# Sliding-window attention with a gated feed-forward: the last 128 output rows in three pieces instead of two

## The chip, the cores and the metric

The kernel runs on one core of a Trainium2 chip. The time is the device time of one execution in microseconds (us), given as the median of several executions. The profile comes from one execution of its own, and its span (first to last recorded instruction) is a little shorter than that execution's time.

## The reference

Causal attention in a window of 64 positions, for 8 batches, 8 heads, 576 positions and 64 values per head; its output, reordered to 4608 rows (tokens) of 512, goes through a gated feed-forward layer with a hidden width of 1536. Cut to what matters:

```python
scores = np.where((rel >= 0) & (rel < 64), scale * (q @ k.T), -1e9)   # rel: query minus key position
attn = softmax(scores) @ v                                            # per batch and head
x = attn.transpose(0, 2, 1, 3).reshape(4608, 512)
gate = np.maximum(x @ w_gate, 0.0)
val = x @ w_val
out = (gate * val) @ w_out                                            # 4608 x 512, float32
```

## The kernel before, in words

The 4608 rows are cut into ten tiles: four of 384 rows and six of 512. For each tile `t` the kernel computes attention into `xt` (inputs in 16 bits, transposed), then `hidden(t)`, then `output(t)`.

`hidden` runs over the 12 blocks of 128 hidden columns (`NF` = 12): four matmuls with `wg` and four with `wv` for each block (L468). ScalarE applies the ReLU to the first result (L453), VectorE multiplies it by the second into `g_sb` (L456).

`output` runs over the 128-row groups of the tile, called `sub`. For each group one tile `op` of 128 x 512 in PSUM, the accumulator memory, takes 12 matmuls of 512 columns (L482), which add up the 12 hidden blocks. `out_evac` then copies `op` to `o_sb` in SBUF, the working memory, on ScalarE (L489), and SP, an engine that only issues transfers here, starts the store to `out` (L490).

The instruction order on each engine is written out by hand (`tc.manual_schedule()`). A small planner, `Weaver`, keeps a clock that advances with each planned matmul; work on other engines is put in with a due time (`W.at`) and is emitted when the clock gets there. `W.drain()` emits all that is left.

The last of the ten tiles goes through `output_last`: its first three groups as above, then `W.drain()`, then the fourth group, the last 128 rows, in pieces of its own. Before the change there are two pieces of 256 columns, each in an `op` tile of its own with 12 matmuls (L514). The first piece is copied by ScalarE and stored from SP's queue. The second is copied in two halves of 128 columns: one by ScalarE, stored from ScalarE's queue, and one by VectorE, stored from SP's queue (copies L520, stores L521).

Two pools matter. `op` tiles come from `f_ps` under the tag `h`, four banks of PSUM used in turn, together with the `h` tiles of `hidden`. `o_sb` tiles come from `f_sb`, three buffers used in turn: a copy into a buffer has to wait until the store that last read it has landed. The pool `consts`, with one buffer for each name, never reuses a tile.

Of the kernel before, what the change touches and what calls it, by code (L numbers as in the profile page):

```python
# [10 lines left out]
FP32 = mybir.dt.float32  # L11
# [33 lines left out]
def kernel(  # L45
# [10 lines left out]
    nc = tc.nc  # L56
    B, H, S, D = q.shape
    DM = H * D
# [14 lines left out]
    starts = [TT * t for t in range(NS)] + [NS * TT + WT * t for t in range(NL)]  # L73
    widths = [TT] * NS + [WT] * NL

    consts = ctx.enter_context(tc.tile_pool(name="consts", bufs=1))
# [6 lines left out]
    f_sb = ctx.enter_context(tc.tile_pool(name="f_sb", bufs=3))  # L83
# [5 lines left out]
    wo = persist.tile([128, NF, DM], FP16)  # L89
# [403 lines left out]
    def op_tile():  # L493
        return f_ps.tile([128, DM], FP32, name="op", tag="h")

    def output(t, subs=None):
        for sub in range(widths[t] // 128) if subs is None else subs:
            op = op_tile()
            for f in range(NF):
                if f % 4 == 0:  # L500
                    W.advance(W.clock)
                out_mm(t, op, sub, f)
            out_evac(t, op, sub)

    def output_last(t):

        last = widths[t] // 128 - 1
        output(t, range(last))
        W.drain()
        for col in range(2):  # L510
            op = op_tile()
            for f in range(NF):
                g_sb, _ = gs[t]
                nc.tensor.matmul(op[:, 0:256], g_sb[:, f, bass.ds(last * 128, 128)], wo[:, f, 256 * col:256 * col + 256],  # L514
                                 start=(f == 0), stop=(f == NF - 1))
            parts = ((0, 256, nc.scalar.copy, nc.sync),) if col == 0 else (
                (0, 128, nc.scalar.copy, nc.scalar), (128, 256, nc.vector.tensor_copy, nc.sync))
            for c0, c1, copy, queue in parts:
                o_sb = f_sb.tile([128, DM], FP32, name="o_sb")
                copy(o_sb[:, c0:c1], op[:, c0:c1])  # L520
                queue.dma_start(out[bass.ds(starts[t] + last * 128, 128), 256 * col + c0:256 * col + c1], o_sb[:, c0:c1])  # L521

    def output_by_rows(t):
        ops = [op_tile() for _ in range(TT // 128)]
# [8 lines left out]
    with tc.manual_schedule():  # L533
# [134 lines left out]
        for t in range(2, NS + NL):  # L668
            ready(t)
            ahead(t)  # L670
            hidden(t, ((0, widths[t]),))
            (output if t < NS + NL - 1 else output_last)(t)
# [31 lines left out]
```

The softmax here doesn't subtract the row's maximum and nothing guards it: scores larger than these inputs give would overflow.

## Time and profile before

| | |
|---|---|
| time, median of 8 executions | 325.11 us (324.96 to 327.58) |
| the profiled execution, its own time | 325.25 us |
| its span in the profile | 323.5 us |
| mean granted TensorE clock | 0.989 of full |
| busy: TensorE, VectorE, ScalarE, GpSimd | 97%, 59%, 39%, 29% of the span |
| start of the last group's matmuls | 317.40 us |

In the lines of the profile PE is TensorE's matmuls and PEld its weight loads, DVE is VectorE, ACT ScalarE, POOL GpSimd and SP SyncE; a q behind the name is the engine's instruction queue, whose own instructions (issuing a transfer, waiting on a semaphore) are not counted as busy. L514 is line 514 of the kernel. A timeline line gives start, duration, engine, line and operation, then the tiles as out<-in, how many instructions were merged, and in brackets how long the engine had been idle and what released it. The chain is the work that ended last, followed backwards from step to step. A line of issues gives the number of transfers, their size and the time from issue to landing.

### The profile page before, as it was taken

The page shows a single profiled execution, that of the slowest core. Times are in us where ns is not written, and L with a number is a line of the kernel's source. Part 1 is how long each engine was busy: PE and PEld are TensorE (multiplying, and loading weights), DVE is VectorE, ACT ScalarE, POOL GpSimd, SP SyncE. Part 2 cuts the span into 40 slices and gives each one's busy share as a digit, 9 for nine tenths or more (in the row PEclk, how much of TensorE's full clock was granted, in tenths as well). Part 3 has the DMA queues.
Part 4 walks back from the last instruction along what each step waited for, and adds up shares of the span by engine and source line. Part 5 has one row for each costly group of instructions (what it writes and reads, how often), then busy time and mean ns, then how long its engine had stood idle before and what let it go on. Part 6 is the DMA issues. An engine that isn't in the chain of part 4 may idle for free.

```text
span 323.5 us, 8901 instructions
## 1 busy us (share of the span) xinstructions
PE 314.6 (97%) x3851; PEld 169.0 (52%) x3851; DVE 192.0 (59%) x370; ACT 126.9 (39%) x249; POOL 93.6 (29%) x138
## 2 busy tenths in 40 slices
PE   6699999999999999999999999999999999999995
PEld 2585958656556644454445444454445444544443
DVE  5947972587838759564765656673767146723410
ACT  3444325534424523542354234613372237223321
POOL 8766335296800290029100920081000000000000
PEclk9699999999999999999999999999999999999999
DMA  8999998989590079009900892091001200020002
GB/s 217 187 195 210 194 103 175 154 149 163 90 203 4 9 105 190 3 8 125 216 5 4 108 210 18 2 121 71 0 2 37 97 0 2 18 111 6 0 34 98
DMA packets 52488, 29.48 MB, mean 91 GB/s; under 512 B 38880, under 2 KB 43872, under 8 KB 52448
## 3 DMA queue, kind: packets, MB, share of 16 engines
q0 software_dynamic: 46688, 18.29, 48.1%
q1 hardware_dynamic: 5616, 10.55, 9.0%
q8 instruction: 30, 0.49, 0.6%
q14 instruction: 10, 0.08, 0.1%
q10 hardware_dynamic: 144, 0.07, 0.1%
HBM read 37.75 MB, written 9.44 MB: 146 GB/s over the span
## 4 chain that ended last, share of the span: by engine, by line
PE 94%; DMA 2%; POOL 2%; issue 0%; ACT 0%; DVE 0%; DVEq 0%; POOLq 0%
PE h L468 59%; PE op L482 28%; PE st L233 3%; PE pv L371 2%; DMA v<-in_v_dram 2%; PE pv L293 1%; POOL v L191 1%; DMA out_dram<-o_sb 1%; POOL k L167 0%; POOL v L202 0%; POOL v L200 0%; ACT o_sb L489 0%; POOL q L167 0%; PE st L207 0%; POOL ident L107 0%
## 5 line engine op out<-in xcount | busy, mean ns | idle before, releaser
L456 DVE TENSOR_TENSOR g_sb<-r_sb,h 128x512 f16<-128x512 f32 (+1 forms) x120 | 75.3, 630 | 86.5 <-PE h L468 84.8
L468 PE MATMUL h<-xt,wg 128*128 128x512 f16 (+2 forms) x544 | 112.8, 339 | 0.1
L468 PE MATMUL h<-xt,wv 128*128 128x512 f16 (+2 forms) x544 | 111.3, 336 | 0.0
L453 ACT ACTIVATE r_sb<-h 128x512 f32<-128x512 f32 (+1 forms) x120 | 66.7, 558 | 89.8 <-PE h L468 83.9
L482 PE MATMUL op<-wo,g_sb 128*128 128x512 f16 x420 | 93.9, 379 | 0.0
L468 PEld LDWEIGHTS <-wg 128*128 128x128 f16 x544 | 51.9, 99 | 42.7 <-issue 0.6
L468 PEld LDWEIGHTS <-wv 128*128 128x128 f16 x544 | 50.5, 98 | 40.8
L482 PEld LDWEIGHTS <-g_sb 128*128 128x128 f16 x420 | 40.3, 98 | 47.1
L191 POOL DMA_DIRECT2D v<-in_v_dram x41 | 34.6, 863 | 95.1 <-PE pv L371 90.1
L489 ACT COPY o_sb<-op 128x512 f32<-128x512 f32 x35 | 20.5, 585 | 84.7 <-PE op L482 84.5
L356 DVE TENSOR_TENSOR pw<-pw,mask 128x512 f16<-128x512 f16 x48 | 19.3, 422 | 14.7 <-ACT pw L352 14.3
L352 ACT ACTIVATE pw<-st 128x512 f16<-128x512 f32 x48 | 25.7, 607 | 5.0 <-PE st L233 4.7
L200 POOL COPY v<-v 64x512 f16<-64x512 f16 (+1 forms) x21 | 15.4, 732 | 24.0 <-DMA v<-in_v_dram 23.2
L185 DVE STREAM_TRANSPOSE kT<-k 128x576 f32<-128x576 f32 x16 | 19.9, 1246 | 0.2 <-ACT k L178 0.2
L185 DVE STREAM_TRANSPOSE qT<-q 128x576 f32<-128x576 f32 x16 | 19.3, 1237 | 0.1
L267 ACT ACTIVATE p<-st 128x384 f16<-128x384 f32 (+1 forms) x40 | 14.0, 442 | 8.2 <-PE st L233 8.2
L391 DVE TENSOR_TENSOR xw<-pv,rw 128x448 f16<-128x448 f32 (+1 forms) x36 | 16.2, 506 | 0.4
L202 POOL COPY v<-v 64x512 f16<-64x512 f16 (+1 forms) x21 | 15.9, 758 | 1.0
L233 PEld LDWEIGHTS <-kT 32*128 32x128 f16 x1152 | 10.8, 94 | 10.1 <-issue 7.9
L233 PE MATMUL st<-qT,kT 32*128 32x64 f16 x1152 | 12.9, 192 | 3.0 <-DVE qT L185 3.0
L396 DVE STREAM_TRANSPOSE xt<-xw 128x1024 f16<-128x1024 f16 x12 | 14.9, 1244 | 0.4
L272 DVE TENSOR_TENSOR p<-p,mask 128x384 f16<-128x384 f16 x24 | 9.1, 398 | 3.5 <-ACT p L267 3.4
(46 smaller groups left out, 99.0 us busy)
## 6 DMA issues: line engine op xcount, KB each, us to landing
out_dram<-o_sb SPq DMA_DIRECT2D x35, 256.0 KB, 2.7
k<-in_k_dram POOLq DMA_DIRECT2D x15, 288.0 KB, 5.3
q<-in_q_dram POOLq DMA_DIRECT2D x15, 288.0 KB, 7.9
v<-in_v_dram POOLq DMA_DIRECT2D x31, 128.0 KB, 8.7
wg<-in_moe_w_gate_dram POOLq DMA_DIRECT2D x6, 256.0 KB, 6.4
wv<-in_moe_w_val_dram POOLq DMA_DIRECT2D x6, 256.0 KB, 8.2
wo<-in_moe_w_out_dram POOLq DMA_DIRECT2D x3, 512.0 KB, 12.1
v<-in_v_dram POOLq DMA_DIRECT2D x10, 64.0 KB, 6.0
```

The costliest lines, as they stand in the source:

```text
L185: nc.vector.transpose(dst.rearrange("p (i j) -> p j i", i=32)[:, j0:j1], src[:, j0:j1])
L191: nc.gpsimd.dma_start(v16s[b % 2][lo:hi, g, :, 0:64], v[b, :, 64 * g - 64 + lo:64 * g - 64 + hi].rearrange("h p d -> p h d"))
L202: copy(t[0:64, g0:g1:2, h0:h1, 0:64], t[64:128, g0 - 1:g1 - 1:2, h0:h1, 0:64])
L233: return [lambda dh=dh: nc.tensor.matmul(to, kTs[b % 2][rows, hh, 64 * w:64 * w + 128, dh], qTs[b % 2][rows, hh, 64 * w:64 * w + 64, dh], ...
L352: nc.scalar.activation(d["p"][g].rearrange("p n c -> p (n c)"), d["st"][g], ACT.Exp, scale=scale)
L356: nc.vector.tensor_tensor(p, p, mask[:, None, :].to_broadcast([128, 2 * QW, 64]), MUL)
L391: nc.vector.tensor_tensor(d["x"][:, hh, s0:s1], pv[:, :, 0:D].rearrange("p s (c e) -> p s e c", e=2), d["r"][:, hh, s0:s1, :, None].to_bro ...
L453: nc.scalar.activation(part(r_sb), part(h1), ACT.Relu)
L456: nc.vector.tensor_tensor(g_sb[:, f:f + w, c0:c0 + n], part(r_sb), part(h2), MUL)
L468: nc.tensor.matmul(h[:, b * n:b * n + n], wt[:, c, (f + b) * 128:(f + b) * 128 + 128], xt[:, c, c0:c0 + n], start=(c == 0), stop=(c == NC ...
L482: nc.tensor.matmul(op, g_sb[:, f, bass.ds(sub * 128, 128)], wo[:, f], start=(f == 0), stop=(f == NF - 1))
L489: nc.scalar.copy(o_sb, op)
```

## The change

The last 128 rows are computed in three pieces of 256, 128 and 128 columns, 12 matmuls each. The first two are copied whole by ScalarE and stored from SP's queue. The third is copied in two halves of 64 columns: one by ScalarE, stored from ScalarE's queue, one by VectorE, stored from SP's queue. Each of the four copies writes a tile of its own from `consts`, exactly as wide as it is, in place of a part of an `o_sb` buffer.

```diff
         last = widths[t] // 128 - 1
         output(t, range(last))
         W.drain()
-        for col in range(2):
+        for c0, c1 in ((0, 256), (256, 384), (384, DM)):
             op = op_tile()
+            n = c1 - c0
             for f in range(NF):
                 g_sb, _ = gs[t]
-                nc.tensor.matmul(op[:, 0:256], g_sb[:, f, bass.ds(last * 128, 128)], wo[:, f, 256 * col:256 * col + 256],
+                nc.tensor.matmul(op[:, 0:n], g_sb[:, f, bass.ds(last * 128, 128)], wo[:, f, c0:c1],
                                  start=(f == 0), stop=(f == NF - 1))
-            parts = ((0, 256, nc.scalar.copy, nc.sync),) if col == 0 else (
-                (0, 128, nc.scalar.copy, nc.scalar), (128, 256, nc.vector.tensor_copy, nc.sync))
-            for c0, c1, copy, queue in parts:
-                o_sb = f_sb.tile([128, DM], FP32, name="o_sb")
-                copy(o_sb[:, c0:c1], op[:, c0:c1])
-                queue.dma_start(out[bass.ds(starts[t] + last * 128, 128), 256 * col + c0:256 * col + c1], o_sb[:, c0:c1])
+            halves = ((0, n // 2, nc.scalar.copy, nc.scalar), (n // 2, n, nc.vector.tensor_copy, nc.sync))
+            for i, (a0, a1, copy, queue) in enumerate(halves if c1 == DM else ((0, n, nc.scalar.copy, nc.sync),)):
+                o_sb = consts.tile([128, a1 - a0], FP32, name=f"o_last{c0}_{i}")
+                copy(o_sb, op[:, a0:a1])
+                queue.dma_start(out[bass.ds(starts[t] + last * 128, 128), c0 + a0:c0 + a1], o_sb)
```

## The prediction

> **What bounds the kernel now.** I read the page's busy line and its chain first, then the chain of waits and the timeline of the last microseconds, then the stores' times to landing.
>
> ```profile
> PE 314.6 (97%) x3851; PEld 169.0 (52%) x3851; DVE 192.0 (59%) x370; ACT 126.9 (39%) x249; POOL 93.6 (29%) x138
> ...
> PE 94%; DMA 2%; POOL 2%; issue 0%; ACT 0%; DVE 0%; DVEq 0%; POOLq 0%
> ```
>
> TensorE is busy for 97% of the span and makes 94% of the chain that ended last. The change touches only what follows 317.2 us, so the question is how long TensorE's last 24 matmuls take and what runs after them. The chain in order of time, over the last stretch:
>
> ```profile
> 317.60 0.59 ACT o_sb L489
> 318.19 0.02 issue
> 318.21 2.00 DMA out_dram<-o_sb
> 320.20 0.03 issue
> 320.23 0.05 DVEq L520
> ...
> 320.62 0.29 DVE o_sb L520
> ```
>
> The last VectorE copy is tied to a store: the one of the third 128-row group, issued at 318.21 and landed at 320.20. The copy's `o_sb` is the same one of the pool's three buffers. After the landing VectorE's queue works through four semaphore instructions, about 0.1 us apart, and copies at 320.62. The timeline of the same stretch:
>
> ```profile
> 317.18 2.71 PEld L514 LDWEIGHTS <-g_sb 128*128 128x128 f16 x24
> 317.40 2.78 PE L514 MATMUL op<-wo,g_sb 128*128 128x256 f16 x24
> 317.60 0.58 ACT L489 COPY o_sb<-op 128x512 f32<-128x512 f32 x1 [2.00 <-PE op L482]
> 318.95 0.37 ACT L520 COPY o_sb<-op 128x256 f32<-128x256 f32 x1 [0.77 <-PE op L514]
> 319.35 1.92 SPq L521 DMA_DIRECT2D out_dram<-o_sb  x2
> 320.26 0.27 ACT L520 COPY o_sb<-op 128x128 f32<-128x128 f32 x1 [0.94 <-PE op L514]
> 320.56 0.37 ACTq L521 DMA_DIRECT2D out_dram<-o_sb  x1
> 320.62 0.29 DVE L520 COPY o_sb<-op 128x128 f32<-128x128 f32 x1 [10.03 <-ACT o_sb L520]
> ```
>
> TensorE ends at 317.40 + 2.78 = 320.18. ScalarE's copy of the last half runs from 320.26 to 320.53; VectorE's starts only at 320.62, and its bracket names ScalarE's copy as the releaser, not the store. So two things hold it: the store's landing with the semaphores behind it (until 320.57), and ScalarE's copy (until 320.53). A copy released by ScalarE starts some 0.03 us after it elsewhere (ACT L352 from 273.06, 0.61 long by its row's mean, then DVE L356 at 273.69). ScalarE alone would thus have let it start at 320.56: **the buffer's wait costs 0.06 us, not the 10 us in the bracket.** The issues in section order:
>
> ```profile
> out_dram<-o_sb SPq DMA_DIRECT2D x3, 256.0 KB, 2.0
> out_dram<-o_sb SPq DMA_DIRECT2D x1, 128.0 KB, 1.7
> out_dram<-o_sb ACTq DMA_DIRECT2D x1, 64.0 KB, 1.6
> out_dram<-o_sb SPq DMA_DIRECT2D x1, 64.0 KB, 1.7
> ```
>
> SP issues VectorE's half at 320.94 (the second of the merged SPq row: 319.35 + 1.92 - 0.33), which lands at 320.94 + 1.7 = 322.64. ScalarE's half lands at 320.56 + 1.6 = 322.16. The span closes at 323.5, 0.86 after the later one. The end is: TensorE, ScalarE copy, VectorE copy, SP's store, closing.
>
> **What the Trainium skill says.** "PSUM — Partial Sum Buffer", section "PSUM bank collisions raise a hardware error", says that two engines must be kept off one bank at once, two readers included. The trace agrees in kind: the halves share `op` and are copied one after the other. "TensorE: Matmul & The Clock Gate", section "Wait — 56ns, not 53.3ns?", gives N/2.4 + 2.5 ns from one warm matmul to the next, so 55.8 ns for 128 columns. The trace agrees at every width that it has: 192 columns 82.5 ns (below), 512 columns 215.8 (the 36 of L482 from 309.63 to 317.40). The same page, "Back-to-back issue gap", gives about 81 ns for pairs of weight load and matmul at 128 columns; its figure beside that, 131 ns at 512, is not what this trace shows. "DMA: Bandwidth & Descriptors", "Specifications", says that below 512 bytes a transfer does a read-modify-write; no store of before has such short rows.
>
> **The change part by part.**
>
> *Matmuls.* Before, 24 of 256 columns at 109.2 ns (256/2.4 + 2.5): the last starts at 317.40 + 23 x 0.1092 = 319.91 and takes 0.27. After, 12 of 256 columns, then 24 of 128. No 128-column row of this shape exists in the trace. Its nearest rows:
>
> ```profile
> 18.76 2.80 PE L468 MATMUL h<-xt,wv 128*128 128x192 f16 x32
> 21.40 2.76 PE L468 MATMUL h<-xt,wg 128*128 128x384 f16 x16
> ...
> 26.70 0.55 PE L233 MATMUL st<-qT,kT 32*128 32x64 f16 x48
> 27.18 2.77 PE L468 MATMUL h<-xt,wg 128*128 128x384 f16 x16
> ```
>
> The 192-column ones, with a weight load each, come every (21.40 - 18.76)/32 = 82.5 ns, the bare streaming price, although a weight load shows 97 ns: loads overlap each other and hide at 82.5. The L233 ones, 128-column weights on 32 rows, come every 0.48/48 = 10 ns, four row groups in parallel, so one group is reloaded every 40 ns. A load's spacing therefore lies between 40 and 82.5 ns; I take 55.8, streaming. A 128-column matmul lasts about 0.22 (273 ns at 256, 379 at 512, same slope). The end moves to 317.40 + 12 x 0.1092 + 23 x 0.0558 + 0.22 = 320.21: **+0.03 us**. At 82.5 ns it would be +0.64; less than +0.03 is excluded by streaming.
>
> *First and middle pieces.* Columns 0 to 256 run as before: copy 318.95, SP issue 319.35 to 319.68. The middle piece's last matmul ends at 318.71 + 11 x 0.0558 + 0.22 = 319.54; ScalarE, free since 319.32, copies from 319.62 to 319.89 (265 ns), and SP issues from 319.92 to 320.25. That one added copy and one added issue lie under the third piece's matmuls. If that cover went, they would cost 0.27 on ScalarE and 0.33 on SP, which has 0.5 us to spare before its last issue. The added store is 64 KB and lands before the last. Nothing is moved past on other queues, POOL is idle here, and the two later `op` tiles need banks whose copies ended by 315.6.
>
> *Last piece.* ScalarE starts 0.08 after the end, at 320.29. Its copies are 585, 372 and 265 ns at 512, 256 and 128 columns, 0.83 ns a column, so 64 take 0.21: until 320.50, issue at 320.53 (0.03 earlier than before). In the list of waits of the changed program as built, VectorE's copy waits for ScalarE's alone; the waits for eight store semaphores are gone. It starts at 320.53 and takes 0.29 less 64 columns of about 1 ns (L391: 614 ns at 448, 292 at 128), 0.23: until 320.76. SP issues at 320.79, not 320.94: **-0.15 us** including the matmuls' +0.03. Of it 0.06 is the buffer, 0.12 the two narrower copies in series.
>
> *The last store.* Half the bytes, in rows of 256 bytes. 64 KB lands no sooner than 128 KB does (1.7 both on SP, 1.6 on ScalarE's queue), so fewer bytes are worth 0 to -0.1. The read-modify-write: 9 packets an engine of about 25 ns (144 packets are 1.2% of 16 engines over the 19 us queried) are 0.23 us, and a doubling would add as much. Its issue also overlaps ScalarE's by 0.1 us (320.53 to 320.90 against 320.79), where before they just missed. I take +0.05, with -0.1 and +0.3 as ends.
>
> **Sum:** -0.15 + 0.05 = -0.10 us. The profiled execution took 325.25 (span 323.5 and 1.75 around it), so 325.15; the median of the runs is 325.11, 0.14 below, so 325.0.
>
> **The rivals.**
> - *Weight loads set the pace* (slower). For it: LDWEIGHTS shows 97 ns against 55.8, and the skill's 81. Against it: 40 ns in a row group, and full hiding at 192 columns. It turns the gain into a loss from 55.8 + 100/23 = 60 ns a matmul. At 81 ns TensorE ends 23 x 0.025 = 0.58 later than in my sum: 325.6. At 97 ns, 0.95 later: 325.95.
> - *The 256-byte store lands late* (about even). At +0.3 the sum is +0.15: 325.3.
> - *The tail was worth more* (faster). If the 32 KB land 0.3 sooner, as 128 KB do against 256: 324.7. Two copies truly side by side would start VectorE at 320.29 and give another 0.24, but its wait on ScalarE's copy excludes that; so the words "by two engines" do not mean at once, before or after.
> - *It does nothing*: narrower copies and the shorter wait are eaten by the end's fixed 1.7 + 0.86 us: 325.1.
>
> **How the numbers follow.** A measurement of this kernel can tell about 0.3% from no change, 0.98 us; all these cases lie inside. Chances: small gain as worked out, with the case of nothing, 0.60 (324.8 to 325.2); weight loads 0.16; late store 0.12; more gain 0.08; something outside this list, either way, 0.04. The range 324.6 to 325.7 leaves out the worst weight-load case and the unlisted. Faster by over 0.3%: 0.04; slower by over 0.3%: 0.05, mostly weight loads near or above 97 ns; the rest within.
>
> **What would show it.** In the changed profile: 24 matmuls of 128 columns in about 1.5 us, TensorE's end near 320.2; ScalarE copies of 0.21 and VectorE's of 0.23 us, starting 0.03 after ScalarE's ends and with no semaphore instructions of its queue ahead; SP's last issue near 320.8, landing in 1.6 to 1.8; the same 0.86 after. I am wrong if those matmuls take 2 us or more, if VectorE starts beside ScalarE, if the last store takes over 2 us, or if anything before 317 us moves.

## The result and the profile after

The changed kernel takes 325.62 us (median of 21 executions) against 325.04 us for the kernel before (60 executions): 1.0016 of its time, 95% interval 1.0009 to 1.0022, so 0.58 us slower. The forecast was 0.1 us faster. The measured time lies inside the range of 324.6 to 325.7 and inside the 0.3% that the prediction counts as no change, but the change makes the kernel slower and not faster.

The timeline of the changed kernel from 317 us on (start, duration, engine, line, what was done):

```profile
316.99 2.85 PEld L515 LDWEIGHTS <-g_sb 128*128 128x128 f16 x36
317.20 2.81 PE L515 MATMUL op<-wo,g_sb 128*128 128x256 f16 x36
317.40 0.58 ACT L489 COPY o_sb<-op 128x512 f32<-128x512 f32 x1 [2.00 <-PE op L482]
...
318.71 0.37 ACT L520 COPY o_last<-op 128x256 f32<-128x256 f32 x1 [0.72 <-PE op L515]
319.11 1.77 SPq L521 DMA_DIRECT2D out_dram<-o_last  x3
319.38 0.27 ACT L520 COPY o_last<-op 128x128 f32<-128x128 f32 x1 [0.30 <-PE op L515]
320.05 0.21 ACT L520 COPY o_last<-op 128x64 f32<-128x64 f32 x1 [0.41 <-PE op L515]
320.29 0.37 ACTq L521 DMA_DIRECT2D out_dram<-o_last  x1
320.29 0.22 DVE L520 COPY o_last<-op 128x64 f32<-128x64 f32 x1 [9.91 <-ACT o_last L520]
```

TensorE's last 36 matmuls take 2.81 us where the 24 of before took 2.78. ScalarE's copy takes 0.21, VectorE's starts 0.03 after it and takes 0.22, SP issues the last store at 320.54. The whole last group began 0.20 earlier in this execution (317.20 against 317.40), so distances from that start are compared below. The last store's time to landing, and the page's first line:

```profile
out_dram<-o_last SPq DMA_DIRECT2D x1, 32.0 KB, 1.5
```

```profile
span 323.8 us, 8922 instructions
```

From the group's start the store is issued after 3.34 us (3.54 before), it lands 1.49 later (1.67 before), and yet the span ends 6.62 after the group's start (6.12 before). Up to the last landing the changed kernel is thus 0.37 us faster, although its matmuls take 0.03 longer. The loss, 0.88 us, lies **between the last landing and the end**: 1.79 us, where it was 0.92.

In that stretch SP closes the program. It waits for the stores' semaphores one after the other (L699, the end of the program, shown in the profile under the line that starts it). What SP waited for from 320 us on, in the kernel before and then in the changed one (us in total, how often, the longest):

```profile
SPq L521 <- DVE o_sb L520: 1.2, 1, 1.2
SPq L699 <- DMA out_dram<-o_sb: 0.8, 2, 0.4
```

```profile
SPq L699 <- DMA out_dram<-o_last: 1.1, 1, 1.1
...
SPq L521 <- DVE o_last L520: 0.5, 1, 0.5
```

Before, the closing stood still twice, for two stores in turn; after, once, for one store, and everything else comes behind it. The count of SP's wait instructions in short windows shows where. Behind the count stand the shortest, median and longest duration in ns, then the first and the last start. Before, from 321.3 to 321.8 and from 322.15 to 322.65:

```profile
L699 SPq EVENT_SEMAPHORE  x7: 17/28/28, 321.3 to 321.7; - x7
...
L699 SPq EVENT_SEMAPHORE  x2: 28/28/28, 322.2 to 322.6; - x2
```

After, from 320.5 to 321.9, 322.0 to 322.3, and 322.65 to 322.95:

```profile
L699 SPq EVENT_SEMAPHORE  x1: 17/17/17, 320.9 to 320.9; - x1
...
L699 SPq EVENT_SEMAPHORE  x4: 28/28/28, 322.0 to 322.3; - x4
...
L699 SPq EVENT_SEMAPHORE  x4: 28/28/28, 322.7 to 322.9; - x4
```

Before, seven of nine waits are done while the last stores are still under way. After, one is; eight follow the last landing at 322.03. The first of the nine waits names no store. The other eight, with the semaphore that each names, from the trace's records:

```
          before                          after
semaphore wait passed  landed      wait passed  landed
108       321.37       289.12      322.04       322.03  <- last store
111       321.44       291.76      322.11       291.57
113       321.50       315.05      322.18       314.84
114       321.59       317.63      322.25       317.43
115       321.67       320.21      322.69       320.00
116       321.74       321.03      322.77       320.81
117       322.19       322.15      322.84       321.24
118       322.62       322.60      322.91       321.85
                       ^ last store
```

The transfers that SP and ScalarE issue take these eight semaphores in rotation. Before, there are 40 of them (SP's two loads at the start and 38 stores), five full rounds, so the last store has the eighth semaphore, the last that SP asks for. The change adds one store, from four to five in the end stretch, so the last store gets the first semaphore. SP stands at it and then has seven more waits to go through, all satisfied by then, from 322.04 to 322.91. They come about 0.07 us apart, but one, that for 115, comes 0.44 after the one ahead of it, although its store landed at 320.00.

### The profile page after: what moved, and what is told of

It reads as the page before. It is cut to its first block, busy times and chain, and to the rows that moved or that the text cites. A ratio compares the mean times of both kernels' runs of the same rounds, so it can differ in the third digit from the quotient of the medians.

```text
span 323.8 us, 8922 instructions
## 1 busy us (share of the span) xinstructions
PE 314.1 (97%) x3863; PEld 168.8 (52%) x3863; DVE 192.5 (59%) x370; ACT 127.1 (39%) x250; POOL 93.6 (29%) x138
## 4 chain that ended last, share of the span: by engine, by line
PE 95%; POOL 2%; DMA 2%; issue 0%; DVE 0%; ACT 0%; POOLq 0%
PE h L468 59%; PE op L482 28%; PE st L233 3%; PE pv L371 2%; DMA v<-in_v_dram 2%; PE pv L293 1%; PE op L515 1%; POOL v L191 1%; POOL k L167 0%; POOL v L202 0%; POOL v L200 0%; POOL q L167 0%; PE st L207 0%; POOL ident L107 0%; POOL ident L111 0%
## 5 line engine op out<-in xcount | busy, mean ns | idle before, releaser
L272 DVE TENSOR_TENSOR p<-p,mask 128x384 f16<-128x384 f16 x24 | 9.8, 428 | 3.4 <-ACT p L267 3.2
```

## The experiments

The theory, **closing order**: the loss is the number of waits that stand behind the last store in SP's fixed order, plus one slow wait at a fixed place of SP's program. Rivals: the rows of 256 bytes, more transfers as such, the two queues or engines at the end. Runs named after_ change the changed kernel, runs named before_ the kernel before. Each run's time is compared with that of the kernel before in the same session (median 325.04 us, for after_384 and whole_64 325.12).

### The last store's semaphore moved, the end left as it is

In after_p7, after_p2 and before_p1, earlier stores are split, seven, two and one of them; the end stretch is untouched.

```diff
+    SPLIT = [(t, sub) for t in (5, 6) for sub in range(4)][:7]   # or 2, or 1
...
-            nc.sync.dma_start(out[bass.ds(starts[t] + sub * 128, 128)], o_sb)
+            cut = 256 if (t, sub) in SPLIT else 0
+            for c0, c1 in ((0, cut), (cut, DM)) if cut else ((0, DM),):
+                nc.sync.dma_start(out[bass.ds(starts[t] + sub * 128, 128), c0:c1], o_sb[:, c0:c1])
```

> The kernel before, with one earlier store split in two. Its end is computed, copied and stored as before; only the semaphores rotate by one, so that the last store has the first semaphore of SP's closing order. 'Closing order': SP waits for that store first, then goes through seven more waits (0.5 us) and the slow one (0.37): 0.85 us slower than before, 325.9. 'Short rows': there are none, 325.0. 'More transfers cost': at most a few hundredths, 325.1.

Measured: 325.78 us, 1.0024 of before (1.0015 to 1.0032). The end of the kernel before, with one store more in the middle, loses 0.74 us. From its trace, SP's waits from 322.7 to 323.1 and from 323.48 to 323.7 (the lines of this copy of the file are four higher):

```profile
L703 SPq EVENT_SEMAPHORE  x5: 28/28/28, 322.8 to 323.1; - x5
...
L703 SPq EVENT_SEMAPHORE  x3: 28/28/28, 323.5 to 323.6; - x3
```

Again all eight follow the last landing (322.74), with the gap of 0.44 in them. No short rows, no third piece, no tiles of their own: the loss of the change is made without any of it.

> The changed kernel with two earlier stores split in the same way. 'Closing order': the last store now has the third semaphore, five remain behind it in the order (0.35 us at 0.07 each), and SP's slow wait (about 0.37 us extra, at a fixed place in SP's program) lies ahead of the landing and is hidden: 0.5 us faster than the changed kernel, 325.1, level with before. If only the number of waits behind the last store counts and the slow wait moves along: 325.45. 'Short rows' and 'more transfers cost': 325.6 or more.

Measured: 325.16 us, 1.0004 of before (0.9996 to 1.0012). So 0.46 of the changed kernel's 0.58 is gone. In its trace the slow wait meets the last store's own semaphore (landed 321.93, passed at 322.15), and five waits follow. So it isn't hidden, as was expected, but costs about 0.2 us.

> The changed kernel with seven earlier stores of 256 KB (row groups of two tiles, at some 155 to 225 us) each issued as two of 128 KB, nothing else. Theory 'closing order': SP closes the program by waiting for eight store semaphores one after the other in a fixed order, and they are given to stores in rotation. With seven more stores the last store gets the last semaphore again, as before the change, and SP's one slow wait falls into the middle of the kernel. The span then ends 0.9 us after the last landing instead of 1.8: 0.85 us faster than the changed kernel, 324.7 us, faster than before. Rival 'short rows': the 256-byte rows of the last two stores end the program late; nothing changes, 325.6. Rival 'more transfers cost': each further store on SP adds a little; 325.6 or more.

Measured: 325.25 us, 1.0009 of before (1.0001 to 1.0017): 0.37 faster than the changed kernel, not 0.85. The closing does what was expected: the last store landed at 322.51, its wait passed at 322.52, the span ended 0.91 after the landing. But the last two stores landed late, 2.0 us after issue instead of 1.5. The transfers of its trace from 320.2 to 320.6 (issues), and from 320.9 to 321.9 (queues: packets, MB, share of 16 engines):

```profile
out_dram<-o_last ACTq DMA_DIRECT2D x1, 32.0 KB, 2.0
out_dram<-o_last SPq DMA_DIRECT2D x1, 32.0 KB, 2.0
```

```profile
q10 hardware_dynamic: 144, 0.03, 15.2%
q1 hardware_dynamic: 144, 0.03, 15.0%
q14 instruction: 1, 0.01, 3.4%
```

One packet of queue 14 (q14 above, of the kind instruction), 8 KB, ran for 0.54 us (3.4% of 16 engines over 1 us) just where the last stores were moved. In the changed kernel that packet came at 323.3, after them. Whether it was the cause was asked next.

### The same semaphore without a longer program on SP

after_act7 splits the same seven stores and issues the second halves from ScalarE's queue; after_p6 splits six, on SP.

```diff
-                nc.sync.dma_start(out[...], o_sb[:, c0:c1])
+                (nc.scalar if c0 else nc.sync).dma_start(out[...], o_sb[:, c0:c1])   # after_act7
```

> The changed kernel with seven earlier stores split as in after_p7, but each second half is issued from ScalarE's queue, so that SP's program keeps its length. The last store has the last semaphore. 'Closing order' with 'the 0.45 us that after_p7's last stores landed late came from an instruction fetch of 8 KB that fell beside them': without that fetch there the last store lands 1.5 us after its issue and the span ends 0.9 later: 324.7 us. 'A last store on the last semaphore always lands late with 256-byte rows': 325.2 as in after_p7. If seven issues of 0.37 us on ScalarE disturb the middle: above 325.2.

Measured: 324.75 us, 0.9991 of before (0.9984 to 0.9998). The last store landed in 1.5 us, the instruction packet came at 323.0, the span ended 0.92 after the landing. With seven transfers more it is 0.87 us faster than the changed kernel.

> The changed kernel with six earlier stores split, all on SP. The last store has the seventh of eight semaphores, one wait (0.07 us) stands behind it. If the fetch goes with the length of SP's program, one instruction less than in after_p7 leaves it beside the last stores: 325.2 to 325.3. If it doesn't fall there: 324.8.

Measured: 325.39 us, 1.0006 of before (0.9997 to 1.0015), 0.1 more than expected. The packet fell from 321.12 to 321.77. In the trace's records 120 of the 128 row packets of ScalarE's store had started by 321.43; the other eight, a sixteenth, started from 321.77 on, just as it ended. In after_p7 eight of the 128 likewise started from 321.57 on, where its packet ended. The records don't name the engine of a packet, but this fits one of sixteen that carried the instruction packet, and stores that waited for it. It explains a part: of the 0.67 us that the last store landed later than in the changed kernel (0.48 in after_p7), 0.35 (0.17) lie before the end of its last packet, and 0.3 in both runs after it. Why that rest grew is not shown.

The traces do show what sets the packet's place. In all twelve it starts 0.57 to 0.65 us after the eightieth of SP's recorded instructions, the one that is slow: in the changed kernel at 323.35 after 322.69, in after_p7 at 321.04 after 320.42. Stores added on SP's queue bring the eightieth instruction forward to the last stores, and the packet with it; in after_act7, with the second halves on ScalarE's queue, it stays behind them (323.00 after 322.37).

### One store fewer

after_384 leaves the last 128 columns as the change has them, but makes one piece of the first 384.

```diff
-        for c0, c1 in ((0, 256), (256, 384), (384, DM)):
+        for c0, c1 in ((0, 384), (384, DM)):
```

> The changed kernel in two pieces of 384 and 128 columns: the last 128 columns as in the change (two halves of 64, tiles of their own, rows of 256 bytes, two queues), one store fewer, so the last store has the last semaphore with no store added or split anywhere. 'Closing order': as after_act7, 324.7 us, 0.9 faster than the changed kernel. 'Short rows' or 'two queues at the end': near 325.6.

Measured: 324.98 us, 0.9995 of before (0.9987 to 1.0004): 0.64 faster than the changed kernel, with the same short rows on the same two queues, but 0.3 short of the expectation. The last store landed in 1.65 us instead of 1.49. The 1536-byte rows of the first piece (on SP's queue from 320.62 to 321.31) were all but through when its own packets started at 321.30, and 0.14 of the added 0.17 us lie after its last packet; why is not shown. The first piece's landing (321.67) held SP's wait for 116, and the slow wait came only after it (passed 322.14), past the last landing at 322.11.

after_whole keeps three pieces and gives the third to ScalarE alone.

```diff
-            for i, (a0, a1, copy, queue) in enumerate(halves if c1 == DM else ((0, n, nc.scalar.copy, nc.sync),)):
+            for i, (a0, a1, copy, queue) in enumerate(((0, n, nc.scalar.copy, nc.sync),)):
```

> The changed kernel, but its third piece of 128 columns is copied whole by ScalarE (0.27 us) and stored from SP's queue in one transfer with rows of 512 bytes: one store fewer, so the last store has the last semaphore. 'Closing order': SP issues 0.38 us after the last matmul (0.75 in the kernel before), lands 1.65 later, closes 0.9 later: 0.35 us faster than before, 324.7. 'Short rows': also faster than the changed kernel, near 325.0. 'Two engines at the end are needed': no faster than before, 325.0 or more.

Measured: 324.62 us, 0.9986 of before (0.9979 to 0.9992), below both kernels. Its timeline:

```profile
317.31 2.81 PE L515 MATMUL op<-wo,g_sb 128*128 128x256 f16 x36
...
319.21 1.56 SPq L521 DMA_DIRECT2D out_dram<-o_last  x3
319.49 0.27 ACT L520 COPY o_last<-op 128x128 f32<-128x128 f32 x1 [0.30 <-PE op L515]
320.15 0.27 ACT L520 COPY o_last<-op 128x128 f32<-128x128 f32 x1 [0.40 <-PE op L515]
```

and what SP waited for at the closing:

```profile
SPq L699 <- DMA out_dram<-o_last: 0.3, 1, 0.3
```

One copy of 0.27 replaces 0.21 + 0.22 in series, the last store is issued 0.33 us after TensorE's end (0.53 in the changed kernel), and SP's slow wait (from 321.13 to 321.58) lies ahead of the landing at 322.10.

whole_64 narrows the last piece further.

```diff
-        for c0, c1 in ((0, 256), (256, 384), (384, DM)):       # in after_whole
+        for c0, c1 in ((0, 256), (256, 448), (448, DM)):
```

> after_whole with pieces of 256, 192 and 64 columns, each copied whole by ScalarE. Last copy 0.21 instead of 0.27 us, rows of 256 bytes. If 64-column matmuls run at the streaming pace (29 ns) the end moves by -0.05 us: 324.57. If weight loads set their pace at 40 ns, TensorE ends 0.13 later than that: 324.7; at 56 ns or more 324.9 or more. Its 12 last starts give the spacing directly.

Measured: 324.76 us, 0.9988 of before (0.9981 to 0.9995), no gain over after_whole. TensorE is not the reason:

```profile
L515 PE MATMUL op<-wo,g_sb x36: 192/246/273, 318.0 to 320.6; 128*128 128x256 f16 x12, 128*128 128x192 f16 x12, 128*128 128x64 f16 x12
```

Its 36 matmuls again take 2.81 us; with 109.2 and 82.5 ns for the wider ones, the 64-column ones came every 29 ns. What took the gain was SP's queue: it was still issuing the middle piece (320.81 to 321.14) when the last copy ended at 321.02.

### The tiles of their own

```diff
-                o_sb = f_sb.tile([128, DM], FP32, name="o_sb")
+                o_sb = consts.tile([128, DM], FP32, name=f"o_last{col}_{c0}")   # before_own: in the kernel before
...
-                o_sb = consts.tile([128, a1 - a0], FP32, name=f"o_last{c0}_{i}")
+                o_sb = f_sb.tile([128, DM], FP32, name="o_sb")[:, 0:a1 - a0]    # after_pool: in the changed kernel
```

> The kernel before, only with tiles of their own for its last three copies; pieces, stores and semaphores as before. The prediction's reading: VectorE's copy starts 0.03 us after ScalarE's instead of 0.09, the last store is issued 0.06 earlier: 324.98 us, not to be told from before. Rival 'the buffer wait is worth what the bracket and the chain of before suggest' (the landing at 320.20, then 0.4 us of semaphore instructions): 324.6.

Measured: 324.89 us, 0.9995 of before (0.9987 to 1.0003); in the trace VectorE's copy starts 0.03 after ScalarE's end (0.09 before), and ScalarE's last copy 0.04 after TensorE's (0.08 before, where a semaphore instruction for a buffer's store stands ahead of that copy, too). The last store is issued 0.10 earlier, and the group's start to the end of the span is 0.09 shorter than before.

> The changed kernel with its four copies in the shared pool of three o_sb buffers instead of tiles of their own. With four copies the fourth, VectorE's, gets the buffer of the first piece, whose store lands 320.8 - and then goes through two or three semaphore instructions of 0.1 us: it starts near 321.1 instead of 320.29. The closing order is as in the changed kernel: 0.8 us slower than that, 326.4. If own tiles don't matter: 325.6.

Measured: 326.37 us, 1.0038 of before (1.0026 to 1.0051). The timeline line of its last copy:

```profile
321.38 0.22 DVE L520 COPY o_sb<-op 128x64 f32<-128x64 f32 x1 [10.78 <-DMA out_dram<-o_sb]
```

VectorE waits for the first piece's store (landed 321.06) and three semaphore instructions. By the traces and the medians, tiles of their own are worth 0.1 us with two pieces and 0.75 with four copies over three buffers.

### All of them together

The first column is read from each trace: from the last group's first matmul to the end of the span, less the same in the kernel before (6.12 us). The second is the difference of the medians.

| kernel | semaphore of the last store | trace, us | medians, us |
|---|---|---|---|
| after | first | +0.50 | +0.58 |
| before_p1 | first | +0.76 | +0.74 |
| after_pool | first | +1.34 | +1.33 |
| after_p2 | third | +0.18 | +0.12 |
| after_p6 | seventh, packet beside | +0.36 | +0.35 |
| after_p7 | eighth, packet beside | +0.11 | +0.21 |
| after_act7 | eighth | -0.40 | -0.29 |
| after_384 | eighth | -0.14 | -0.14 |
| before_own | eighth | -0.09 | -0.15 |
| after_whole | eighth | -0.40 | -0.42 |
| whole_64 | eighth | -0.39 | -0.36 |

The two columns agree within 0.11 us: what these kernels gain and lose is made after 317 us, in the stretch that the trace shows.

## Why the prediction was wrong

**Matmuls: right.** +0.03 us was forecast, +0.03 measured; 128-column matmuls stream at 55.8 ns. The slower rival, weight loads, is refuted more widely than it was argued: even 64 columns, with a load each, stream at 29 ns in whole_64, below the 40 that the prediction read as the least for a load. That its price at 81 ns would have given just the measured 325.6 is chance.

**First and middle pieces: wrong.** The added store was costed at nothing, "under the third piece's matmuls". Its copy (319.38 to 319.64) and its issue do lie there. What it moved was neither: the last store's place in the rotation of semaphores. This is the step that failed, together with the sentence that "the same 0.86" follows the last landing. The closing (0.92 by the records) was taken as fixed; it depends on which semaphore lands last. Term by term: forecast 0, measured +0.88. before_p1, which moves the last store to the first semaphore and leaves the end's copies and stores as they were, shows the same loss alone (1.81 us from the last landing to the end, 0.92 before).

**Last piece: right, a little small.** -0.15 was forecast to SP's issue, -0.19 measured. VectorE's copy does follow ScalarE's, as was read from the wait list. The reading that the buffer's wait costs hundredths and not what the chain suggests holds too, but 0.06 is VectorE's part alone: ScalarE's copy was taken to start 0.08 after TensorE's end as before, and with tiles of its own it starts 0.04 after it (before_own, and the changed kernel). That is the 0.04 by which the term fell short.

**The last store: wrong sign.** +0.05 was forecast, -0.18 measured: 32 KB in rows of 256 bytes landed in 1.5 us, 64 KB in rows of 512 in 1.67. In the records a packet of 256 bytes takes 18 ns and one of 512 bytes 27, so the doubling that the prediction allowed for isn't there. No run supports the rival of the late store: 256-byte stores landed late in after_p6 and after_p7 alone, with the instruction packet beside them. The overlap of the two issues shows no harm.

The sum thus becomes -0.19 - 0.18 + 0.88 = +0.51 in the profiled executions (read directly, +0.50), where -0.10 was forecast. None of the rivals held the mechanism, which falls under the 0.04 for something outside the list, although the profile before shows SP's closing waits, and the added store was known: the last store's semaphore could have been counted. The part of the trace after the last landing was taken as a constant because it was the same work; its order was left out of account.

## What to carry to other kernels

A program's end has a part after the last landing, and it is not a constant: here SP asked for eight store semaphores in a fixed order, and one store more moved the last store from the last place of that order to the first, worth up to 0.9 us. When an end stretch is tuned for tenths, count the transfers that share those semaphores and let the last store have the one that is asked for last, before judging the pieces themselves. Splitting the last copy between two engines brought nothing here, where they follow one another: after_act7, which splits it, and after_whole, which doesn't, end alike in their traces (-0.40 us both), each with its last store on the eighth semaphore. One copy by one engine, with one store fewer, gets there without stores split elsewhere.

## What the runs showed of the hardware

- In SP's closing, satisfied waits come 0.06 to 0.10 us apart, but the eightieth of SP's recorded instructions comes 0.44 to 0.45 us after the one ahead of it wherever no landing or copy holds it longer (after, before_p1, after_p2, after_whole, after_act7, after_384, whole_64, after_pool). It stays with the count of instructions and not with the semaphore. In the kernel before, the same wait passed at 322.19, 0.45 after the one ahead of it, but the last store landed only at 322.60, so it cost nothing.
- One instruction packet of 8 KB starts 0.57 to 0.65 us after that instruction in all twelve traces, so it goes with SP's program. A fetch of instructions for SP would fit both; what happens in the slow instruction itself was not settled, and no run tested it.
- Where that packet ran beside the last stores (0.54 us in after_p7, 0.65 in after_p6), they landed in 2.0 to 2.2 us instead of 1.5. A sixteenth of their row packets started only when it had ended.
